# An adaLN block on one core: a new order ahead of the first exponential, and the first 512 tokens normed in two pairs

## The chip, the core and the metric

One core of a Trainium2 chip. TensorE (PE) multiplies, with its weight loads (PEld) listed apart; VectorE (DVE), ScalarE (ACT) and GpSimd (POOL) do the rest; SyncE (SP) issues the DMA transfers, one after the other in the order of the program. Each engine works through its own instructions in order. The metric is the device time of one execution in microseconds (us), compared as medians of several runs.

## What is computed

One transformer block for 2048 tokens of 512 values in float32, with 32 heads of 16 and a feed-forward width of 1792. Cut to what matters:

```python
mod = (_silu(c) @ w_mod).reshape(c.shape[0], 6, 1, -1)
sa, ca, ga, sb, cb, gb = (mod[:, 0], mod[:, 1], mod[:, 2], mod[:, 3], mod[:, 4], mod[:, 5])
h = _layernorm(x, axis=-1) * (1 + ca) + sa
x = x + ga * _A_ref(h, A_wqkv, A_wo)      # softmax attention over all tokens
h = _layernorm(x, axis=-1) * (1 + cb) + sb
x = x + gb * _B_ref(h, B_w1, B_b1, B_w2)  # dense, mish, dense
```

## The kernel before

Products in the projections are made in three parts: each float32 operand is split into a high part (rounded to the format that PE takes at full rate) and a low part (the rest), and high x high, high x low and low x high are added. `hi_copy` (L91 to L95) makes the high part on ACT, DVE or POOL; `lo_sub` (L98) subtracts to get the low part. `mm3` queues the three groups of products of one unit, `mm_go` (L129) issues one of them on PE.

*Prologue, one block of 512 tokens (tb) after the other.* x comes in as 16 tiles of 128 tokens (`xt`, L334). `stats_tb` takes mean and variance of four tiles on DVE (L371, L372) and makes the scale and shift `rs` on POOL (L373 to L376; L375 is the inverse square root as a power). `apply_tb` norms the four tiles on ACT (L382). `tr_tb` transposes them on PE, column by column of 128 values (L388: column k of all four tiles goes to one PSUM bank), applies the modulation `modc`, and writes the high part `h_h` (ACT, L391), the full value `hf` (DVE, L392) and the low part `h_l` (L98). `modc` comes from products of `w_mod` with the activated condition (L400, L404, L406) and two small DVE instructions (L410, L411). The weights stand in slices of 128 columns for queries (kind 0) and keys (kind 1) and 256 for values (kind 2); `slice_load` loads one (L231), `slice_split` splits it. `qk_unit` makes keys or queries of one slice for 512 tokens: 12 products 512 wide. Its `fin` splits the result and stores it to DRAM scratch (L269 for queries, three transfers; L273 and L274 for keys). `v_unit` does the same for values: 12 products 256 wide per 128 tokens.

*The 20 steps ahead of the first exponential (t = -20 to -1).* Softmax needs a row maximum first. In each step `max_pair` makes two pairs of score products (four times L494) that DVE reduces (L496); the rest of the step is filled with products of the queued units by `whole_units`. A step is allowed `CREDIT` products of width 512, two of width 256 counting as one, and the count starts anew in each step. When the next unit is not ready, what is left of the credit is lost. At t = -4 the maxima of the first four heads are complete: PE transposes them (L509), ACT and DVE split them (`mh` L511, `mt` L512), and one step later four small transfers (L518) put them into rows 48 and 49 of the query tiles `qa`, which the first score products (L529) read.

*The 512 steps behind.* Each makes four score products with their exponentials (L529, L532), the products of two steps earlier with the values (L547), and four maxima of the next group of four heads (L480, L482); units of the projections and of the rest of the block fill in.

What is done when is set by hand. `at(h, f)` puts f at half step h = 2t, or 2t + 1 for the second half of a step; `plan` lists the units in their order. When a unit of the plan is finished, the split of the slice two entries on is put at the next half step, the load of the slice three entries on one or two half steps later. A unit of the plan may start four half steps after the split of its slice:

```python
queue(lambda i=i, t=t0: max(2 * t, split_at.get(i, 4 * T) + 4), lambda tag, i=i, a=a: planned(i, a, tag))
```

`early_prep` loads, splits and stores six pieces of w1 in these 20 steps (L1393, L1401). `constants` stores zeros to the scratch rows 48 and 49 and loads the bias (L417 to L419), at the end of the prologue. POOL's fills of the later key tiles (L460) wait for memory that these transfers read.

## Time and profile before

| | us |
|---|---|
| median of 3 runs | 1699.01 |
| lowest and highest | 1698.46, 1699.34 |
| the profiled execution, its own time | 1697.49 |
| its span, first to last instruction | 1695.7 |
| PE busy in the span | 1672.8 (99%) |
| DVE, ACT, POOL busy | 1437.8, 1358.3, 820.1 |
| first transpose of x on PE (L388) | 15.92 |
| first L494 (maxima) | 50.59 |
| first L529 (scores) | 105.40 |

Times within the profile count from the start of the span. A row of its timeline gives start, length, engine, line and operation, output and inputs, how many instructions were merged, and in brackets the idle time of the engine before it with what ended it.

### The profile page before, as it was taken

The page shows a single profiled execution, that of the slowest core. Times are in us where ns is not written, and L with a number is a line of the kernel's source. Part 1 is how long each engine was busy: PE and PEld are TensorE (multiplying, and loading weights), DVE is VectorE, ACT ScalarE, POOL GpSimd, SP SyncE. Part 2 cuts the span into 40 slices and gives each one's busy share as a digit, 9 for nine tenths or more (in the row PEclk, how much of TensorE's full clock was granted, in tenths as well). Part 3 has the DMA queues.
Part 4 walks back from the last instruction along what each step waited for, and adds up shares of the span by engine and source line. Part 5 has one row for each costly group of instructions (what it writes and reads, how often), then busy time and mean ns, then how long its engine had stood idle before and what let it go on. Part 6 is the DMA issues. An engine that isn't in the chain of part 4 may idle for free.

```text
span 1695.7 us, 33728 instructions
## 1 busy us (share of the span) xinstructions
PE 1672.8 (99%) x12406; PEld 924.7 (55%) x12406; DVE 1437.8 (85%) x2370; ACT 1358.3 (80%) x2612; POOL 820.1 (48%) x838
## 2 busy tenths in 40 slices
PE   7999999999999999999999999999999999999999
PEld 5755665555445455555555455555555455555587
DVE  6888888888899888888889898888889988884378
ACT  6247777777778988888888998888888988888674
POOL 6456223665413464655423564555323564555442
PEclk9999999999999999999999999999999999999999
DMA  6887546777755342534355434434354433433261
GB/s 234 237 274 193 135 127 185 232 218 212 229 170 140 100 107 75 136 80 126 81 155 148 117 74 98 134 72 134 84 142 128 130 93 77 143 107 128 77 230 62
DMA packets 114029, 238.44 MB, mean 141 GB/s; under 512 B 23824, under 2 KB 49424, under 8 KB 107912
## 3 DMA queue, kind: packets, MB, share of 16 engines
q1 hardware_dynamic: 113864, 236.28, 49.3%
q8 instruction: 98, 1.61, 0.4%
q14 instruction: 67, 0.55, 0.1%
HBM read 179.95 MB, written 51.44 MB: 136 GB/s over the span
## 4 chain that ended last, share of the span: by engine, by line
PE 91%; DVE 4%; ACT 2%; DMA 2%; issue 0%; SPq 0%; POOL 0%; ACTq 0%; DVEq 0%
PE bk L547 29%; PE ring L529 23%; PE ring L480 20%; PE bk L136 9%; PE bk L129 3%; PE ring L1156 2%; DVE mx L482 2%; PE ring L129 2%; ACT pr L532 1%; DMA xt<-in_A_x 1%; PE ring L494 1%; DMA qa<-mt 1%; PE ring L859 0%; PE ring L509 0%; DVE hf L392 0%
## 5 line engine op out<-in xcount | busy, mean ns | idle before, releaser
L482 DVE TENSOR_REDUCE mx<-ring 128x1 f32<-128x512 f32 x1968 | 1223.0, 682 | 153.1 <-PE ring L480 137.4
L532 ACT ACTIVATE pr<-ring 128x512 f32<-128x512 f32 x2048 | 1078.3, 602 | 209.1 <-PE bk L136 121.1
L480 PE MATMUL ring<-ka,qa 64*128 64x512 f32 x1968 | 818.8, 430 | 1.6 <-ACT pr L532 1.1
L529 PE MATMUL ring<-qa,ka 64*128 64x512 f32 x2048 | 760.8, 403 | 5.4 <-DMA qa<-mt 2.6
L547 PE MATMUL bk<-pr,vg 128*32 128x512 f32 x4096 | 545.1, 604 | 0.0
L480 PEld LDWEIGHTS ring<-ka,qa 64*128 64x128 f32 x1968 | 351.2, 184 | 327.8 <-DVE mx L482 251.0
L529 PEld LDWEIGHTS ring<-qa,ka 64*128 64x128 f32 x2048 | 374.1, 184 | 199.0 <-DVE mx L482 114.7
L136 PE MATMUL bk<-h,w 64*128 64x512 f32 (+1 forms) x1080 | 278.9, 391 | 0.0
L136 PE MATMUL bk<-w,a_h 64*128 64x512 f32 x632 | 210.6, 413 | 0.0
L136 PEld LDWEIGHTS bk<-h,w 64*128 64x128 f32 x1080 | 178.3, 184 | 9.5 <-ACT pr L532 1.5
L547 PEld LDWEIGHTS bk<-pr,vg 128*32 128x32 f32 x4096 | 80.7, 108 | 136.2 <-issue 126.6
L136 PE MATMUL bk<-w,a_l 64*128 64x512 f32 x316 | 124.1, 393 | 0.0
L136 PEld LDWEIGHTS bk<-w,a_h 64*128 64x128 f32 x632 | 107.0, 184 | 2.2
L915 POOL TENSOR_TENSOR y<-yd,y 128x512 f32<-128x512 f32 x44 | 56.9, 1294 | 89.4 <-ACT yd L914 84.5
L749 POOL TENSOR_SCALAR qq<-ee 128x512 f32<-128x512 f32 x25 | 15.6, 624 | 169.3 <-ACT ee L743 169.3
L765 POOL TENSOR_TENSOR qq<-qq,rr 128x512 f32<-128x512 f32 x42 | 54.3, 1292 | 83.4 <-ACT rr L759 83.3
L751 POOL TENSOR_TENSOR hb<-hb,ee 128x512 f32<-128x512 f32 x42 | 54.2, 1291 | 82.3 <-DVE ee L747 80.4
L136 PE MATMUL bk<-w,o_hl 64*128 64x512 f32 x288 | 79.1, 405 | 0.0
L98 POOL TENSOR_TENSOR a_l<-hb,a_h 128x512 fp32r<-128x512 f32 x53 | 72.1, 1361 | 4.4
L136 PEld LDWEIGHTS bk<-w,a_l 64*128 64x128 f32 x316 | 58.3, 184 | 2.4
L136 PE MATMUL bk<-h_h,wl 64*128 64x512 f32 x168 | 57.7, 425 | 0.0
L95 POOL TENSOR_SCALAR qh<-qf 128x512 fp32r<-128x512 f32 x27 | 16.8, 622 | 82.8 <-ACT qf L259 56.3
(210 smaller groups left out, 1909.0 us busy)
## 6 DMA issues: line engine op xcount, KB each, us to landing
ka<-kscr SPq DMA_DIRECT2D x124, 384.0 KB
w<-w2scr SPq DMA_DIRECT2D x56, 512.0 KB
w<-w1scr SPq DMA_DIRECT2D x46, 512.0 KB
vg<-vscr SPq DMA_DIRECT2D x32, 552.0 KB
qa<-qscr SPq DMA_DIRECT2D x124, 100.0 KB
kscr<-qh SPq DMA_DIRECT2D x16, 512.0 KB
qscr<-qh SPq DMA_DIRECT2D x32, 256.0 KB
w2scr<-hl SPq DMA_DIRECT2D x14, 512.0 KB
```

Source lines behind the costliest of these rows:

```text
L98: (nc.gpsimd if eng == "p" else nc.vector).tensor_sub(lo, src, hi.bitcast(F32))
L129: nc.tensor.matmul(acc, l, r, start=start, stop=stop)
L136: i = nc.tensor.matmul(acc, l[64 * g:64 * g + 64], r[64 * g:64 * g + 64], start=start and not then, stop=bool(stop and then))
L480: nc.tensor.matmul(pm, qt[64 * s:64 * s + 64, qs * P:(qs + 1) * P], kt[64 * s:64 * s + 64, kb * TB:(kb + 1) * TB], start=True, stop=True)
L482: nc.vector.tensor_reduce(out=mxs[n][:, s, 4 * j + qs, kb:kb + 1], in_=pm, op=ALU.max, axis=AX.X)
L529: nc.tensor.matmul(p_, kt[64 * s:64 * s + 64, kc * P:(kc + 1) * P], qt[64 * s:64 * s + 64, :], start=True, stop=True)
L532: e = nc.scalar.activation(pr, p_, AF.Exp, scale=SCALE)
L547: nc.tensor.matmul(accs[n][32 * h:32 * h + 32, :], vgs[n][:, o:o + 32], pts.pop((t, h)), start=(kc == 0), stop=(kc == 15))
L751: (nc.vector if tail else nc.gpsimd).tensor_mul(hb, hb, ee)
L765: nc.gpsimd.tensor_mul(qq, qq, rr)
L915: nc.gpsimd.tensor_add(y[i], yd, y[i])
L1156: nc.tensor.matmul(po[i // 2][:, i % 2, :], l[:, s], w[:, r, :], start=(f == 0 and j == 0), stop=(f == FT - 1 and j == 2))
```

## The change

Four things move; the numbers of the computation stay the same.

1. `whole_units` carries its credit from step to step (`owed`), 7.4 a step instead of 7.5.
2. The plan takes the second slice of queries ahead of the second slice of keys; loads and splits of later slices get fixed half steps (`LATE_SPLIT`, `LATE_LOAD`), and a unit ahead of step 0 may start two half steps after its split. `constants` is called ahead of the blocks, and the early preparations start three half steps sooner.
3. `first_norm`, `first_apply` and `first_tr` replace `stats_tb(0)`, `apply_tb(0)` and the first transposes: scales for tiles 0 and 1, then for 2 and 3; tile 3 is normed on DVE instead of ACT; tiles 0 and 1 are transposed singly, then 2 and 3 together. The high part of the first key weights is made on POOL between the two pairs.
4. In the first block the products of keys and queries are issued in turn.

```diff
-    CREDIT = 7.5
+    CREDIT = 7.4
+    LATE_SPLIT = {3: -8, 4: 4}
+    LATE_LOAD = {3: -15, 4: -4, 5: 9}
...
-        slice_load(1, 1, pw)
+        slice_load(0, 1, pw)
...
+        def first_norm():
+
+            mv = lp.tile([P, 4, 2], F32, tag="ln_mv4", name="ln_mv4", bufs=2)
+            rs = lp.tile([P, 4, 4], F32, tag="ln_rs4", name="ln_rs4", bufs=3)
+            for h in range(2):
+                two = slice(2 * h, 2 * h + 2)
+                for i in range(2 * h, 2 * h + 2):
+                    st_ = lp.tile([P, 6], F32, tag="ln_st", name="ln_st", bufs=4)
+                    nc.vector.bn_stats(out=st_, in_=xts[i])
+                    nc.vector.bn_aggr(out=mv[:, i, :], in_=st_)
+                nc.gpsimd.tensor_scalar(rs[:, 0, two], mv[:, two, 1], 1.0, EPS, op0=ALU.mult, op1=ALU.add)
+                nc.gpsimd.tensor_scalar(rs[:, 3, two], mv[:, two, 0], -1.0, 0.0, op0=ALU.mult, op1=ALU.add)
+                nc.gpsimd.tensor_tensor(rs[:, 1, two], rs[:, 0, two], nhalf.to_broadcast([P, 2]), op=ALU.pow)
+                nc.gpsimd.tensor_mul(rs[:, 2, two], rs[:, 3, two], rs[:, 1, two])
+                if h == 0:
+                    hi_k = split_hi(1, 0)
+            return rs, hi_k
...
+        def first_apply(rs, i, eng):
+            xt = xts[i]
+            if eng == "a":
+                nc.scalar.activation(xt, xt, AF.Identity, scale=rs[:, 1, i:i + 1], bias=rs[:, 2, i:i + 1])
+            else:
+                nc.vector.tensor_scalar(xt, xt, rs[:, 1, i:i + 1], rs[:, 2, i:i + 1], op0=ALU.mult, op1=ALU.add)
+
+        def first_tr():
+            pts = [bank(("ring", "ms", "ring", "acc")[k]) for k in range(DK)]
+            for ii in ((0,), (1,), (2, 3)):
+                for k in range(DK):
+                    for i in ii:
+                        nc.tensor.transpose(pts[k][:, i * P:(i + 1) * P], xts[i][:, k * P:(k + 1) * P], ident)
+            return pts
...
-        slice_split(1, 0, lp)
-        slice_split(0, 0, lp)
-        apply_tb(0)
+        for i in range(2):
+            first_apply(rs, i, "a")
+        split_lo(1, 0, hi_k)
+        hi_q = split_hi(0, 0, "a")
+        split_lo(0, 0, hi_q)
+        first_apply(rs, 2, "a")
+        first_apply(rs, 3, "v")
...
+            if tb == 0:
+                (kw, qw) = early
+                early = [[m for k in range(DK) for m in (kw[k], qw[k], kw[DK + k])], qw[DK:]]
+            pe_queue.extend(m for e in early for m in e)
...
-        while credit > 0:
+        cur["owed"] = cur.get("owed", 0) + credit
+        while cur["owed"] > 0.49:
...
-    plan = [(-PRO, 2, 0, range(4, 16)), (-PRO, 1, 1, range(NB)), (-PRO, 0, 1, (0,)), (-PRO, 1, 2, range(NB)),
+    plan = [(-PRO, 2, 0, range(4, 16)), (-PRO, 0, 1, (0,)), (-PRO, 1, 1, range(NB)), (-PRO, 1, 2, range(NB)),
...
-                    at(h + d, lambda: slice_split(*plan[i + 2][1:3], hi_eng="p" if h > 0 else "a"))
-                    split_at[i + 2] = h + d
+                    split_at[i + 2] = LATE_SPLIT.get(i + 2, h + d)
+                    at(split_at[i + 2], lambda: slice_split(*plan[i + 2][1:3], hi_eng="p" if h > 0 else "a"))
...
-        at(3 * i - 34, lambda i=i: early_prep(i, 3 * i - 34))
+        at(3 * i - 37, lambda i=i: early_prep(i, 3 * i - 37))
```

How it moves instructions, in the built programs (line numbers of the change are its own; numbers at names tell buffers apart). SP before, around the four transfers of the maxima (L518, mt to qa):

```order
L310 DMA qa_109<-qscr 50x512 x2
L319 DMA ka_626<-kscr 48x2048 x2
L273 DMA kscr<-qh 128x2x512
L274 DMA kscr<-ql 128x512
L231 DMA wr<-in_A_wqkv 128x4x128
L273 DMA kscr<-qh 128x2x512
L274 DMA kscr<-ql 128x512
L518 DMA qa_106<-mt 2x4x128
L518 DMA qa_107<-mt 2x4x128
```

And in the change, where L576 is that transfer, L271 the query store, L275 and L276 the key store, L233 the weight load, L312 and L321 the loads of qa and ka:

```order
L271 DMA qscr<-qh 8x16x512 x2
L271 DMA qscr<-ql 8x16x512
L1461 DMA w1scr<-ep 128x512 x2
L275 DMA kscr<-qh 128x2x512
L276 DMA kscr<-ql 128x512
L312 DMA qa_109<-qscr 50x512 x2
L321 DMA ka_630<-kscr 48x2048 x2
L275 DMA kscr<-qh 128x2x512
L276 DMA kscr<-ql 128x512
L576 DMA qa_106<-mt 2x4x128
L576 DMA qa_107<-mt 2x4x128
L233 DMA wr<-in_A_wqkv 128x4x128
```

The weight load now stands behind the transfers of mt, one key store instead of two stands between the loads of ka and them, and a query store has come in some places ahead.

PE before, the last steps ahead of the first score product (L529; L494 are the maximum products that begin a step, L129 the units):

```order
L494 MATMUL ring<-ka_625,qa_108 128x512 x4
L129 MATMUL bk<-h_l,wh 128x512
L494 MATMUL ring<-ka_625,qa_108 128x512 x4
L129 MATMUL bk<-h_h,wh 128x512 x4
L129 MATMUL bk<-h_h,wl 128x512 x4
L494 MATMUL ring<-ka_625,qa_108 128x512 x4
L129 MATMUL bk<-h_l,wh 128x512 x4
L129 MATMUL bk<-h_h,wh 128x512 x4
L529 MATMUL ring<-qa_106,ka_104 128x512
```

And in the change the same three steps (L552 for L494, L131 for L129, L587 for L529):

```order
L552 MATMUL ring<-ka_629,qa_108 128x512 x4
L131 MATMUL bk<-h_h,wl 128x512 x2
L131 MATMUL bk<-h_l,wh 128x512 x4
L131 MATMUL bk<-h_h,wh 128x512
L552 MATMUL ring<-ka_629,qa_108 128x512 x4
L131 MATMUL bk<-h_h,wh 128x512 x3
L131 MATMUL bk<-h_h,wl 128x512 x4
L131 MATMUL bk<-h_l,wh 128x512
L552 MATMUL ring<-ka_629,qa_108 128x512 x4
L131 MATMUL bk<-h_l,wh 128x512 x3
L131 MATMUL bk<-h_h,wh 128x512 x4
L587 MATMUL ring<-qa_106,ka_104 128x512
```

One, eight and eight products beside the maxima have become seven, eight and seven. The step in front of them, with the transpose of the maxima, has eight in both programs.

DVE before, from the fourth tile's statistics (ln_mv_188 belongs to the first block, ln_mv_241 to the second) to those of the fifth:

```order
L371 BN_STATS ln_st<-xt 128x6
L372 BN_AGGR ln_mv_188<-ln_st 128x2
L410 TENSOR_SCALAR modc<-bk 128x4
L411 COPY modc<-bk 128x4
L371 BN_STATS ln_st<-xt 128x6
L372 BN_AGGR ln_mv_241<-ln_st 128x2
```

And in the change, with the second block's statistics in ln_mv_245:

```order
L394 BN_STATS ln_st<-xt 128x6
L395 BN_AGGR ln_mv_188<-ln_st 128x2
L419 TENSOR_SCALAR xt<-xt,ln_rs_189 128x512
L462 TENSOR_SCALAR modc<-bk 128x4
L463 COPY modc<-bk 128x4
L373 BN_STATS ln_st<-xt 128x6
L374 BN_AGGR ln_mv_245<-ln_st 128x2
```

The norm of tile 3 (L419) has come in ahead of modc and of the second block's statistics; it needs the scales of the second pair.

## The prediction

> **What bounds the kernel now.** I read the page's first line, then the busy time by stage, then the chain of waits from 90 to 110 us, then the timeline of the two stretches in which TensorE (PE) stands idle. By stage (columns: length, then busy time of PE, weight loads, DVE, ACT and POOL with their instructions, granted clock, DMA share, GB/s):

> ```profile
> span 1695.7 us, 33728 instructions
> ```

> ```profile
> 0.00:20.65 20.65, 11.41 (x48) 7.08 (x48) 8.57 (x25) 8.78 (x13) 13.93 (x37) 1.00 0.94 334
> 20.65:50.59 29.94, 28.22 (x158) 22.41 (x157) 25.95 (x41) 22.62 (x35) 17.50 (x19) 1.00 0.50 171
> 50.59:94.00 43.41, 43.41 (x265) 31.88 (x264) 38.57 (x36) 7.91 (x19) 24.79 (x23) 1.00 0.88 267
> 94.00:105.40 11.40, 9.21 (x40) 5.46 (x39) 9.45 (x9) 3.02 (x6) 5.92 (x6) 1.00 0.91 311
> ```

> The first score product (L529, the one the first exponential reads) starts at 105.40. In the built program of the change every PE instruction from that one on stands in the order of before, and ahead of it stand the same products. So PE loses no work, and all that can be won are its waits ahead of L529: 9.24 us idle while x is loaded and normed, 1.72 in the projections, none from 50.59 to 94.00, 2.19 from there on. The end of that stretch, first in the chain of waits (start, length, what), then in the timeline:

> ```profile
> 90.70 0.66 PE ring L494 x4
> 91.36 2.05 PE bk L129 x8
> ...
> 101.08 4.19 DMA qa<-mt
> ```

> ```profile
> 93.34 0.73 PE L494 MATMUL ring<-ka,qa 64*128 64x512 f32 x4
> ...
> 94.00 0.28 PE L509 MATMUL ring<-ident,mm 128*32 128x128 f32 x1
> ...
> 96.08 0.73 PE L494 MATMUL ring<-ka,qa 64*128 64x512 f32 x4
> 96.17 0.33 DVE L512 SCALAR_TENSOR_TENSOR mt<-mh,lows,ring 32x128 fp32r<-32x128 f32 x1
> ...
> 97.90 0.50 PE L494 MATMUL ring<-ka,qa 64*128 64x512 f32 x2 [0.22 <-DVE mx L496]
> 98.21 1.28 POOL L98 TENSOR_TENSOR wl<-wr,wh 128x512 fp32r<-128x512 f32 x1
> ...
> 99.53 0.38 SPq L231 DMA_DIRECT2D wr<-in_A_wqkv  x1
> 99.55 0.76 PEld L129 LDWEIGHTS bk<-h_h,wl 128*128 128x128 f32 x4 [0.45 <-POOL wl L98]
> ...
> 105.40 0.47 PE L529 MATMUL ring<-qa,ka 64*128 64x512 f32 x1 [1.96 <-DMA qa<-mt]
> ```

> The negated maxima mt are ready at 96.50, but their four transfers (L518) start at 101.08. They stand on SP behind a weight load (L231) that waits until POOL's subtraction (98.21 + 1.28 = 99.49) frees its buffer. They land at 105.27, and L529 waits for them. Two more waits lie ahead: the step at 96.08 had a single product beside its four maximum products, so PE ran into DVE at 97.90, and at 99.55 it waited for POOL's weights.

> How much is lost: from 93.34 to 105.40 are 12.06 us. In them PE does four quartets of L494 (0.66 each), 25 products 512 wide (2.05 / 8 = 0.256 each) and L509, for which the step from 93.34 to 96.08 is only some 0.03 longer than the 2.71 of a quartet and eight products: 2.64 + 6.40 + 0.03 = 9.07. **Lost: 2.99 us.**

> **Part 1, the stretch ahead of the first exponential.** With the credit carried over, the 20 steps get seven or eight products each, none only one. In the new order three quartets and 30 products stand between L509 and L529: 1.98 + 7.68 = 9.7 us. The other arm from L509: mt done 2.50 later (96.50 less 94.00), then 4.19 to land, 6.7 us. So L529 no longer waits for mt, by 3.0 us, if L518 can be issued when mt is ready. Ahead of it on SP there is now the store of one K unit only. That unit ends ten products and two quartets ahead of L509 (3.9 us), and needs an ACT copy and two POOL instructions after that, about 0.6 + 0.62 + 1.28 = 2.5 us (the last two by the rows below): ready 1.4 us ahead of L509, 3.9 ahead of mt. The weight split that PE waited for at 99.55 now stands ahead of L509 in the same step, and the half in question is first used one and a half steps behind. DVE has two reduces a step:

> ```profile
> 85.75 2.36 DVE L496 TENSOR_REDUCE mx<-ring 128x2 f32<-128x1024 f32 x2 [0.32 <-PE ring L494]
> ```

> Twenty steps are 47.2 us of DVE; PE's own work in them is 105.40 - 50.59 - 2.99 = 51.8, so DVE does not become the bound; a step with seven products, 0.66 + 1.79 = 2.45, still covers 2.36. I take the whole 2.99. Bounds: 0 if the queue gains nothing, 3.0 if all goes as here; there is no more to win.

> The zero constants (six transfers), the first early weight preparations and with them POOL's fills of ka move ahead. They lie in gaps of SP and POOL beside a PE that is busy 43.41 of 43.41 us; they cost nothing while that cover holds, and uncovered at most SP's own issue time. The split of the fourth slice moves behind the first eight exponentials, one ACT cast of about 0.6 us between exponentials (the one at 24.61 below, of twice the columns, takes 1.04); the slice is used some ten steps later. I take 0.

> **Part 2, the first 512 tokens.** The timeline of before:

> ```profile
> 11.07 3.57 PE L406 MATMUL bk<-sel,row 128*128 128x1 f32 x16
> ...
> 11.41 0.18 DVE L372 BATCH_NORM_AGGREGATE ln_mv<-ln_st 128x2 f32<-128x6 f32 x1
> ...
> 13.27 0.20 POOL L373 TENSOR_SCALAR ln_rs<-ln_mv 128x4 f32<-128x4 f32 x1 [4.52 <-DVE ln_mv L372]
> ...
> 13.70 1.03 POOL L375 TENSOR_TENSOR ln_rs<-ln_rs,nhalf 128x4 f32<-128x4 f32 x1
> ...
> 14.81 0.20 POOL L376 TENSOR_TENSOR ln_rs<-ln_rs 128x4 f32<-128x4 f32 x1
> 14.83 0.68 DVE L371 BATCH_NORM_STATS2 ln_st<-xt 128x6 f32<-128x512 f32 x1
> 14.96 2.50 POOL L98 TENSOR_TENSOR wl<-wr,wh 128x512 fp32r<-128x512 f32 x2
> 15.05 2.93 ACT L382 ACTIVATE xt<-xt,ln_rs 128x512 f32<-128x512 f32 x4 [1.10 <-DMA xt<-in_A_x]
> ...
> 17.93 0.18 DVE L372 BATCH_NORM_AGGREGATE ln_mv<-ln_st 128x2 f32<-128x6 f32 x1
> ...
> 18.55 0.78 ACT L391 ACTIVATE h_h<-ring,modc 128x512 fp32r<-128x512 f32 x1 [0.57 <-PE ring L388]
> ...
> 18.94 0.87 PEld L388 LDWEIGHTS ring<-ident,xt 128*128 128x128 f32 x4
> ...
> 20.25 1.28 POOL L98 TENSOR_TENSOR h_l<-hf,h_h 128x512 fp32r<-128x512 f32 x1 [0.32 <-DVE hf L392]
> ...
> 21.06 1.02 DVE L98 TENSOR_TENSOR h_l<-hf,h_h 128x512 fp32r<-128x512 f32 x1
> ...
> 21.79 2.92 ACT L382 ACTIVATE xt<-xt,ln_rs 128x512 f32<-128x512 f32 x4
> ...
> 24.61 1.04 ACT L91 CAST wh<-wr 128x1024 fp32r<-128x1024 f32 x1
> ...
> 26.08 0.78 ACT L391 ACTIVATE h_h<-ring,modc 128x512 fp32r<-128x512 f32 x1 [0.43 <-PE ring L388]
> ```

> And groups of like instructions (count, then busy time and mean ns):

> ```profile
> L107 POOL TENSOR_TENSOR ln_rs<-ln_rs,nhalf 128x1 f32<-128x1 f32 x16 | 8.9, 554 | 1.3
> L95 POOL TENSOR_SCALAR wh<-wr 128x512 fp32r<-128x512 f32 x6 | 3.7, 620 | 10.7 <-PE bk L136 10.7
> L98 DVE TENSOR_TENSOR h<-hf,h 128x512 fp32r<-128x512 f32 x4 | 2.8, 692 | 2.9 <-POOL h L95 2.9
> L93 DVE CAST a_h<-hb 128x512 fp32r<-128x512 f32 x3 | 1.3, 427 | 0.3
> ```

> *The pairs.* POOL's chain for four tiles runs from 13.27 to 15.01, 1.74 us, with a power of 1.03 on four columns. One column takes 0.554, so two take about 0.71 and a pair's chain 1.42. The first pair's statistics end at 11.59; its scales are ready at 11.68 + 1.42 = 13.10 instead of 15.01. Then POOL copies a weight half (0.62), and the second chain ends at 15.09, no earlier than before. PE is with L406 until 14.64; the eight transposes of tiles 0 and 1 at 0.87 / 4 = 0.22 each then fill it until 16.4. Tile 2 is normed by ACT from 15.13 to 15.9. The first column of tiles 2 and 3 can be transposed at 16.4, and the first h_h starts some 0.8 later, at 17.2 instead of 18.55: 1.3 earlier. The 16 products in turn of keys and queries follow h_h as it comes, and PE is through with them ahead of the next transposes.

> *What is late next.* The next transposes need tiles 4 to 7, and these become later. Their statistics stood at 14.83 on DVE, in a gap; now the norm of tile 3 stands in front of them, waiting for the second chain, with the two modc instructions behind it. If that norm ends at e, the statistics run from e + 0.25 for 3.28 us (14.83 to 18.11), POOL's chain takes 1.8, the four norms on ACT 2.95, the V weights' cast behind them 1.0: the next block's first h_h starts at e + 9.35. Before, it starts at 26.08. So **e = 16.73 is break-even** for that h_h; its transposes and the key and query ends behind it gain about 0.25 more, since before PE and not ACT was late there. Later than 16.73 costs one for one.

> *The price of that norm.* No row shows a DVE scale-and-shift from SBUF to SBUF. The nearest in size and place is the cast of the same shape, 0.43 us, with POOL elsewhere. But in this place POOL starts two subtractions of 1.25 each at the instant DVE is released. The row at 21.06 tells what such a neighbour does: alone that DVE subtraction takes 0.692, beside POOL's (20.25 to 21.53) it took 1.02 and ended 0.55 after POOL. Ends: not held, 15.13 + 0.43 = 15.6, where PE's own 1.0 caps the gain; held through both subtractions, 17.55 + 0.3 = 17.85, a loss of 0.9. I take held through the first only: 15.04 + 1.25 + 0.28 = 16.57, **a gain of 0.16 + 0.25 = 0.4 us**. From there to 50.59 the blocks follow each other as before (PE busy 28.22 of 29.94), so 0.4 arrives.

> [...]

> **Sum.** 2.99 + 0.4 = 3.4 us. The profiled execution took 1697.49 us for its span of 1695.7, so 1694.1 for the like of it; it is 1.5 below the median of the three runs, 1699.01, and against that median I forecast **1695.6 us**. The bound between faster and no change, 0.2%, about what a measurement of this kernel can tell, is 3.4 us as well: the forecast lies on it.

> **Rivals.**
> - *The norm on DVE is not held.* 2.99 + 1.0 = 4.0: 1695.0. For it: DVE may come first. Against: POOL's subtraction waits for nothing and starts at 14.96 in the row, ahead of ACT's 15.05. 0.25.
> - *Held through both.* 2.99 - 0.9 = 2.1: 1696.9. Against: two separate instructions leave DVE a place between. 0.10.
> - *Part 1 gives half.* mt or a weight half still comes late, since DMA is 0.88 to 0.91 busy. 1.5 + 0.4: 1697.1. 0.11.
> - *PE falls to half rate.* In the row at 18.94 a transpose takes 0.22 us, in the one below 0.12, after PE has been busy for some 4 us:

> ```profile
> 25.77 0.47 PEld L388 LDWEIGHTS bk<-ident,xt 128*128 128x128 f32 x4
> ```

>   In the change PE stands nearly idle from about 22.5 to 25, and 4 us at half rate behind that would cost 2: 1.4 in all, 1697.6. [...] 0.06.
> - *The pairs do nothing:* the block waits for tiles 2 and 3 anyway, whose scales come 0.08 later. 3.0: 1696.0. 0.05.
> - *Slower.* L518 stands behind a K store whose high half POOL may write only when the Q unit's stores, two units earlier and now ahead of it, have landed from the same buffer. Each us beyond the spare 3.0 holds PE at L529; past 6.4 us of delay the whole gain is gone, and 10 us give 1702.6. For it: POOL waited so in this stretch. Against: by 2.97 us at most.

> ```profile
> 102.47 0.62 POOL L95 TENSOR_SCALAR qh<-qf 128x512 fp32r<-128x512 f32 x1 [2.97 <-DMA kscr<-qh]
> ```

>   0.06.

> **Numbers.** The forecast's own case has 0.37, half on each side of the bound. Faster: 0.25 + 0.19 and 0.02 of the case in which the pairs do nothing, 0.46. Slower by 0.2%: 0.06. The rest, 0.48, within. The range leaves out the slower case, part of the half-rate one, and the best of the first: 1694.5 to 1697.9.

> **What would show it.** Right: L518 issued within 2 us of mt's end, no wait of PE for mt at L529, seven or eight products in every step, 51.8 us from the first L494 to L529, and the first L494 at about 50.2. The norm of tile 3 on DVE at over 1.2 us beside POOL, the statistics of tile 4 starting near 16.8, the first h_h near 17.2, the next block's first near 26. Wrong: a wait at L529 for the transfer of mt, a DVE norm of 0.5 us or of 2.5, half-rate products behind 25, or a first L494 later than 50.6.

## The result, and the profile after

| | before | the change |
|---|---|---|
| median of 16 runs, us | 1698.49 | 1695.11 |
| lowest and highest | 1696.86, 1699.98 | 1693.99, 1697.61 |
| profiled execution, its time and its span | 1697.49, 1695.7 | 1695.12, 1693.1 |
| first maxima product | 50.59 | 50.30 |
| first score product (L529, now L587) | 105.40 | 102.54 |
| first product with the values (L547, now L605) | 112.42 | 109.29 |

The ratio is 0.9981, 95% interval 0.9975 to 0.9988: 3.4 us faster, 2.0 to 4.2 by the interval. By stage the profile of the change shows (columns as in the prediction's first table):

```profile
20.00:50.30 30.30, 28.17 (x160) 21.99 (x158) 27.07 (x42) 23.23 (x36) 19.84 (x23) 1.00 0.62 190
50.30:102.54 52.24, 52.12 (x304) 37.24 (x303) 47.63 (x44) 9.84 (x22) 29.40 (x28) 1.00 0.87 274
102.54:109.36 6.82, 6.04 (x37) 2.98 (x40) 6.67 (x12) 6.32 (x13) 3.60 (x4) 1.00 0.99 321
```

The second row is the stretch from the first maxima product to the first score product: 52.24 us where it took 54.81, with PE busy for 52.12 of them. The rows around the maxima, from the timeline of the change (L570 makes mt, L576 sends it, L590 are the exponentials):

```profile
92.80 0.09 PEld L567 LDWEIGHTS ring<-ident,mm 128*32 128x32 f32 x1 [0.55 <-DVE mm L561]
...
94.92 0.33 DVE L570 SCALAR_TENSOR_TENSOR mt<-mh,lows,ring 32x128 fp32r<-32x128 f32 x1
95.31 2.79 SPq L576 DMA_DIRECT2D qa<-mt  x4
...
98.73 0.40 SPq L233 DMA_DIRECT2D wr<-in_A_wqkv  x1
...
103.04 0.59 ACT L261 COPY qf<-bk 128x512 f32<-128x512 f32 x1 [5.15 <-PE ring L538]
...
104.18 0.50 PE L587 MATMUL ring<-qa,ka 64*128 64x512 f32 x1 [0.67 <-ACT pr L590]
```

mt is ready at 95.25 and its transfers start at 95.31; L587 no longer waits for them. Two small waits are new: PE is now ahead of DVE at the transpose of the maxima (0.55), and the fourth score product waits for the first exponential, because a copy (L261) stands ahead of it on ACT. The first 27 us:

```profile
3.17 5.58 DVE L361 TENSOR_SCALAR sil_e<-sil_e 128x4 f32<-128x4 f32 x1 [1.51 <-ACT sil_e L360]
...
5.16 3.56 POOL L357 MEMSET ka<- 128x2048 f32 x2
...
15.09 1.47 DVE L419 TENSOR_SCALAR xt<-xt,ln_rs 128x512 f32<-128x512 f32 x1 [2.04 <-POOL ln_rs L399]
...
16.55 0.15 DVE L463 COPY modc<-bk 128x4 f32<-128x4 f32 x1
16.62 0.68 DVE L373 BATCH_NORM_STATS2 ln_st<-xt 128x6 f32<-128x512 f32 x1
...
16.85 0.45 PE L426 MATMUL bk<-ident,xt 128*128 128x128 f32 x1 [0.17 <-DVE modc L463]
...
19.04 0.78 ACT L439 ACTIVATE h_h<-ring,modc 128x512 fp32r<-128x512 f32 x1 [2.90 <-PE ring L426]
...
25.99 0.77 ACT L439 ACTIVATE h_h<-ring,modc 128x512 fp32r<-128x512 f32 x1
```

The norm of tile 3 (L419) takes 1.47 us, the first h_h comes at 19.04, half a microsecond later than before, and the next block's first at 25.99, 0.09 earlier. The first row is a surprise that has nothing to do with the change: an addition on 128x4 values took 5.58 us, up to the end of POOL's fills; before, the same instruction took 0.25.

From L605 on the two programs nearly keep their distance: 1482.0 us to the last product with the values before, 1482.6 in the change.

### The profile page after: what moved, and what is told of

Its sections match the earlier page's. It is cut to its first block, busy times and chain, and to the rows that moved or that the text cites. A ratio compares the mean times of both kernels' runs of the same rounds, so it can differ in the third digit from the quotient of the medians.

```text
span 1693.1 us, 33733 instructions
## 1 busy us (share of the span) xinstructions
PE 1670.7 (99%) x12406; PEld 922.2 (54%) x12406; DVE 1443.6 (85%) x2371; ACT 1356.1 (80%) x2610; POOL 822.3 (49%) x843
## 4 chain that ended last, share of the span: by engine, by line
PE 91%; DVE 4%; ACT 3%; DMA 1%; issue 1%; POOL 1%; SPq 0%; ACTq 0%; DVEq 0%; POOLq 0%
PE bk L605 29%; PE ring L587 22%; PE ring L538 20%; PE bk L138 10%; PE bk L131 3%; PE ring L131 2%; DVE mx L540 2%; PE ring L1214 2%; ACT pr L590 1%; PE ring L552 1%; DMA qa<-mt 0%; DMA xt<-in_A_x 0%; PE ring L917 0%; PE ring L567 0%; PE ring L138 0%
## 5 line engine op out<-in xcount | busy, mean ns | idle before, releaser
L590 ACT ACTIVATE pr<-ring 128x512 f32<-128x512 f32 x2048 | 1078.3, 603 | 207.8 <-PE bk L138 117.9
L587 PE MATMUL ring<-qa,ka 64*128 64x512 f32 x2048 | 760.1, 402 | 4.3 <-ACT pr L590 2.6
L605 PE MATMUL bk<-pr,vg 128*32 128x512 f32 x4096 | 545.0, 604 | 0.0
L587 PEld LDWEIGHTS ring<-qa,ka 64*128 64x128 f32 x2048 | 373.6, 184 | 199.2 <-DVE mx L540 115.2
L605 PEld LDWEIGHTS bk<-pr,vg 128*32 128x32 f32 x4096 | 80.7, 108 | 136.1 <-issue 126.6
L138 PEld LDWEIGHTS bk<-w,a_h 64*128 64x128 f32 x632 | 106.9, 184 | 2.7
L807 POOL TENSOR_SCALAR qq<-ee 128x512 f32<-128x512 f32 x25 | 15.6, 624 | 168.9 <-ACT ee L801 168.9
L97 POOL TENSOR_SCALAR qh<-qf 128x512 fp32r<-128x512 f32 x27 | 16.8, 623 | 88.7 <-ACT qf L261 69.7
```

The source lines that it names most:

```text
L138: i = nc.tensor.matmul(acc, l[64 * g:64 * g + 64], r[64 * g:64 * g + 64], start=start and not then, stop=bool(stop and then))
L587: nc.tensor.matmul(p_, kt[64 * s:64 * s + 64, kc * P:(kc + 1) * P], qt[64 * s:64 * s + 64, :], start=True, stop=True)
L590: e = nc.scalar.activation(pr, p_, AF.Exp, scale=SCALE)
L605: nc.tensor.matmul(accs[n][32 * h:32 * h + 32, :], vgs[n][:, o:o + 32], pts.pop((t, h)), start=(kc == 0), stop=(kc == 15))
```

## The experiments

Each run was timed against the kernel before on the same chip. The times on the right are of one profiled execution each (start of the first maxima product, the first score product, the first product with the values).

| run | ratio to before, 95% | maxima | score | values |
|---|---|---|---|---|
| before | 1 | 50.6 | 105.4 | 112.4 |
| the change | 0.9981 (0.9975 to 0.9988) | 50.3 | 102.5 | 109.3 |
| part 1 alone | 0.9988 (0.9980 to 0.9997) | 50.3 | 102.5 | 109.2 |
| part 2 alone | 0.9998 (0.9989 to 1.0007) | 50.3 | 106.9 | 114.7 |
| addition on ACT | 0.9983 (0.9975 to 0.9992) | 50.2 | 102.4 | 110.6 |
| the same, norm on ACT | 0.9975 (0.9965 to 0.9984) | 48.5 | 102.2 | 109.0 |
| the same, DVE norm alone | 0.9975 (0.9965 to 0.9985) | 49.3 | 101.5 | 108.2 |
| no carried credit | 0.9987 (0.9978 to 0.9996) | 50.3 | 103.9 | 110.4 |
| no tables | 1.0018 (1.0009 to 1.0027) | 50.2 | 109.1 | 117.6 |
| old split, tables of loads kept | 0.9993 (0.9985 to 1.0002) | 50.2 | 103.8 | 110.9 |
| constants and preparations back | 1.0002 (0.9993 to 1.0011) | 50.3 | 104.8 | 112.7 |
| weight load ahead of mt | 0.9980 (0.9971 to 0.9988) | 50.3 | 102.5 | 110.3 |
| mt behind a key store | 0.9994 (0.9985 to 1.0003) | 50.4 | 106.7 | 114.0 |
| three edits more | 0.9964 (0.9952 to 0.9977) | 47.7 | 100.2 | 107.2 |

### The two parts by themselves

Part 1 alone undoes the pairs; part 2 alone puts them into the kernel before.

```diff
-        rs, hi_k = first_norm()
+        stats_tb(0)
...
+        slice_split(1, 0, lp)
+        slice_split(0, 0, lp)
+        apply_tb(0)
...
-        tr_tb(0, pts=first_tr())
+        tr_tb(0)
...
```

> The change without the pairs and without keys and queries in turn: the first 512 tokens are normed, transposed and projected as before; the new plan, the carried credit and the moved constants stay. My theory (the two parts are separate and add up): first maxima product where before has it, 50.6 us; from there to the first score product 52.2 (as in the changed kernel, against 54.8), so that one at 102.8; time 2.6 to 3.0 us under before, 1695.5 to 1696. Rival (the blocks' pairs carry more than their 0.3 us, or the plan needs the blocks' new times): the stretch takes over 53.5 again and the gain is under 1.5 us.

> Before with the pairs, the single transposes and the products in turn alone; plan, credit and constants as before. My theory: first maxima product 0.3 us earlier, at 50.3; the stretch behind it keeps its 54.8 us, with the wait for the transfer of the maxima; first score product at 105.1, time 0.3 us under before. Rival A (the changed kernel was held up in its first 9 us by chance, so that the pairs are worth more): first maxima product at 49.5 or earlier where the condition's activation is not late. Rival B (the pairs only shift a wait): 50.6 and no gain.

Part 1 alone has the whole gain of the stretch: 52.2 us, the first score product at 102.5. It is 2.0 us faster than before (0.5 to 3.4), where 2.6 to 3.0 were expected; the intervals of this run and of the change overlap, so how much of the time the pairs add to part 1 stays open. Part 2 alone is worth 0.3 us, which can't be told from nothing; the wait for mt is there, longer than before (3.64 us at L585). That the first maxima product also comes at 50.3 without the pairs was not expected. The first block's products of keys and queries, first in the timeline of before:

```profile
20.72 2.06 PE L129 MATMUL ring<-h_h,wh 128*128 128x512 f32 x4
22.57 1.17 PE L129 MATMUL ring<-h_h,wl 128*128 128x512 f32 x4
...
25.45 0.60 PE L388 MATMUL ring<-ident,xt 128*128 128x128 f32 x4
```

And in the timeline of part 1 alone:

```profile
12.36 1.95 PE L454 MATMUL bk<-sel,row 128*128 128x1 f32 x16
...
14.49 0.68 DVE L373 BATCH_NORM_STATS2 ln_st<-xt 128x6 f32<-128x512 f32 x1
...
20.67 1.84 PE L131 MATMUL ring<-h_h,wh 128*128 128x512 f32 x4
22.35 1.08 PE L131 MATMUL ring<-h_h,wl 128*128 128x512 f32 x4
...
25.10 0.60 PE L434 MATMUL ring<-ident,xt 128*128 128x128 f32 x4
...
25.73 0.78 ACT L439 ACTIVATE h_h<-ring,modc 128x512 fp32r<-128x512 f32 x1
```

In both runs these products start at nearly the same time, and the next block's transposes follow them on PE. From the first of them to the first transpose it is 4.73 us before and 4.43 here, because PE reached its full rate earlier: by the clock records of the two traces at 22.7 us before and at 22.1 here. The 16 products with sel were faster too (1.95 us, 3.57 before), so that modc and the statistics of tile 4 came 0.34 us earlier; but this did not decide it, since the scales of tiles 4 to 7 were ready at 19.59 and ACT came to norm these tiles at 21.73. So in the old order the next block moves by 0.3 us with the moment at which PE gets its full rate. In the order with the pairs it doesn't: the first maxima product comes at 50.3 to 50.4 whether that moment was at 20.8 us (mt behind a key store) or at 22.7 (part 2 alone), since the norm of tile 3 decides there.

### The norm of tile 3, and who holds DVE

The first of three runs moves the addition that took 5.58 us to ACT; the second norms tile 3 on ACT as well; the third leaves that norm on DVE and lets POOL's first weight subtraction wait for it.

```diff
-        nc.vector.tensor_scalar_add(e, e, 1.0)
+        nc.scalar.activation(e, e, AF.Identity, scale=1.0, bias=ones)
```

```diff
-        first_apply(rs, 3, "v")
+        first_apply(rs, 3, "a")
```

```diff
-        split_lo(1, 0, hi_k)
+        normed = first_apply(rs, 3, "v")
+        sub = split_lo(1, 0, hi_k)
+        tc.add_manual_dep(sub.ins, normed.ins.name, ...)
```

> The change with one instruction moved: the 128x4 addition of 1 in the condition's activation goes from DVE to ACT. In the changed kernel's run this DVE instruction started at 3.17 and lasted 5.58 us, to the end of POOL's fills of the query and key tiles; before it took 0.25 at the same place. Theory (POOL's fills held it out, and this made the first products 2.5 us late, but tile 3's norm and not these products sets the next block): the first products start at 6.7 instead of 9.2, the transposes of the first tiles run before 16.6, the first h_h stands near 17.3 instead of 19.04, and still the next block's first h_h stays at 25.8 to 26.0, the first maxima product at 50.1 to 50.3, the time within 0.3 us of the change. Rival (the late products ate the pairs' gain): the next block's first h_h and the first maxima product come 0.8 us or more earlier, at 49.5.

> As the run before, and tile 3 is normed on ACT instead of DVE. Theory (the DVE norm, held 1.47 us beside POOL's subtraction, makes the statistics of tiles 4 to 7 late): their first one starts at 14.8 to 15.0 instead of 16.62, the next block's first h_h at 24.6 to 25.0 instead of 26.0, the first maxima product near 49.3, the time 1 us under the change, 1694.1. Rival A (behind the first blocks PE or ACT is the bound, the statistics are not): the statistics come earlier, but the first maxima product stays at 50.2. Rival B (ACT, now with one norm more, delays the first h_h by 0.75 and PE with it): 50.6 or later.

> The change with the addition of 1 on ACT (as two runs before) and POOL's first weight subtraction made to wait for the DVE norm of tile 3. Theory (POOL's subtraction held the norm): the norm takes 0.45 to 0.6 us instead of 1.47 and ends at 15.6; the statistics of tile 4 start at 15.7 instead of 16.58, the next block's first h_h at 25.0 instead of 25.93, the first maxima product at 49.3. Rival (a scale and shift of this form takes 1.47 us by itself): the norm ends at 16.5 as before, h_h at 25.9, first maxima product at 50.2. The time is told by neither alone: the run with the norm on ACT gained 1.7 us here and lost 1.5 of it to 3.4 us at half clock, 49.8 to 53.2, behind a wait of 1.06 us.

With the addition on ACT the first products start at 6.56, but the first h_h stays at 18.99: the theory's 17.3 was wrong, the rest of it right (next block's first h_h at 25.93, first maxima product at 50.2). The second transpose waits 2.01 us for modc, in that run's timeline:

```profile
16.80 0.45 PE L426 MATMUL bk<-ident,xt 128*128 128x128 f32 x1 [2.01 <-DVE modc L463]
```

The columns of x go in turn into PSUM banks, and the bank of the second column still holds the product that modc is made from; modc stands behind tile 3's norm on DVE. With that norm on ACT the first h_h starts at 17.20. The rows of the DVE norm, with POOL waiting (timeline of the third run):

```profile
15.02 0.55 DVE L420 TENSOR_SCALAR xt<-xt,ln_rs 128x512 f32<-128x512 f32 x1 [2.04 <-POOL ln_rs L399]
...
15.62 0.68 DVE L373 BATCH_NORM_STATS2 ln_st<-xt 128x6 f32<-128x512 f32 x1
...
24.99 0.77 ACT L440 ACTIVATE h_h<-ring,modc 128x512 fp32r<-128x512 f32 x1
```

0.55 us alone, 1.47 beside POOL's subtraction: the subtraction held it. From the first statistics of tile 4 to the next block's first h_h it is 9.37 us in the change, 9.37 here and 9.40 with the norm on ACT (14.74 to 24.14), so nearly each microsecond of that norm is one of the first maxima product: 50.2, 49.3, 48.5.

Of the 1.7 us that the norm on ACT won by 48.5, 1.5 were gone by the first score product. Its timeline and its stages show where:

```profile
47.56 1.05 PE L131 MATMUL ring<-h_l,wh 128*128 128x512 f32 x2 [1.06 <-POOL h_l L100]
```

```profile
48.50:50.50 2.00, 2.00 (x12) 1.60 (x12) 1.19 (x2) 1.10 (x2) 0.62 (x1) 0.79 0.98 363
50.50:55.00 4.50, 4.50 (x28) 3.70 (x26) 3.79 (x4) 0.68 (x2) 4.50 (x4) 0.71 0.42 128
```

PE waited 1.06 us for a low half, and some 2 us later the granted clock was 0.50 for 3.4 us, 49.7 to 53.1. The change has the same wait of 1.04 at 49.31 and no such fall in its profile; it comes in some executions and not in others.

### The pieces of part 1

Six runs undo one piece each, or shift the transfers of mt.

```diff
-        cur["owed"] = cur.get("owed", 0) + credit
-        while cur["owed"] > 0.49:
+        while credit > 0:
...
```

> The change with the old count of products (each step anew, 7.4): 155 products instead of 148 in the 20 steps, none left out in any step, and one K store more ahead of the transfers of the maxima. Theory (only TensorE's idle time counts; the 7 products more are taken from later steps): the first score product 7 x 0.256 = 1.8 us later, at 104.3, no wait for the maxima there, and the time as the change within 0.5 us: 1695 to 1696. Rival (the carried credit is what gains): the K store, whose half POOL may write only when older stores have landed, stands in front of the maxima's transfers, TensorE waits for them, and the time is 1 us or more above the change.

Without the carried credit the first score product comes 1.4 us later (1.8 expected), as it must with seven products more ahead of it. The theory that they would be won back fails: from L605 to the last product with the values it takes 1482.5 us, 1482.6 in the change. The span is 1.1 us longer, the time 1.0 (the intervals overlap). The rival's K store does stand in front of the maxima: their transfers start at 98.10, 1.9 us behind mt, but by the trace's semaphore events the first of them landed at 103.31, in time for L587. Why the seven products are nearly free in the later steps is not shown.

```diff
-    LATE_SPLIT = {3: -8, 4: 4}
-    LATE_LOAD = {3: -15, 4: -4, 5: 9}
+    LATE_SPLIT = {}
+    LATE_LOAD = {}
...
-                    at(LATE_LOAD.get(i + 3, h + 7), lambda: slice_load(*plan[i + 3][1:3]))
+                    at(LATE_LOAD.get(i + 3, h + (7 if h > 0 else 2)), lambda: slice_load(*plan[i + 3][1:3]))
```

> The change without its tables of half steps for splits and loads (both empty, so the old rule): the same products in the same order, but a weight load stands on SP ahead of the query stores, long before the transfers of the maxima, and waits there for POOL's subtraction. Theory (what gains is the plan's order and the credit; at the maxima 3.0 us are spare): first score product at 102.4 to 102.8, no wait for the maxima, time as the change within 0.5 us. Rival (the tables are what takes the load out of the maxima's way): query and key stores, the loads of the second query and key tiles and the maxima's transfers all start later, TensorE waits 1 us or more in the steps or at the first score product, time 1 us or more above the change.

The rival holds. From the timeline without the tables:

```profile
87.77 1.29 POOL L100 TENSOR_TENSOR wl<-wr,wh 128x512 fp32r<-128x512 f32 x1 [2.45 <-ACT wh L93]
...
89.09 0.38 SPq L233 DMA_DIRECT2D wr<-in_A_wqkv  x1
89.52 1.23 SPq L271 DMA_DIRECT2D qscr<-qh  x2
...
95.88 0.62 POOL L97 TENSOR_SCALAR qh<-qf 128x512 fp32r<-128x512 f32 x1 [4.86 <-DMA qscr<-qh]
...
99.86 0.50 PE L131 MATMUL bk<-h_h,wh 128*128 128x512 f32 x1 [2.75 <-ACT qf L261]
...
101.55 3.75 SPq L576 DMA_DIRECT2D qa<-mt  x4
...
109.12 0.47 PE L587 MATMUL ring<-qa,ka 64*128 64x512 f32 x1 [2.05 <-DMA qa<-mt]
```

Each row releases the next. The weight load waits on SP until POOL's subtraction has read the old slice (87.77 + 1.29), the query stores behind it start at 89.52 instead of 82.77, POOL waits 4.86 us for them to land before it may write the next high part, ACT's copy waits for POOL, PE for that copy, and the maxima leave 6.2 us late. PE loses 2.75 + 2.05 us in waits, half clock follows (below), and the kernel is 6.3 us slower than the change (ratio 1.0018 less 0.9981), slower than before.

```diff
-    LATE_SPLIT = {3: -8, 4: 4}
+    LATE_SPLIT = {4: 4}
```

> The change without the fixed half step for the split of the second slice of keys' successor (the third slice of keys is split by the old rule, some 6 us earlier: ACT's cast and POOL's subtraction ahead of two units' copies); the tables of the loads stay. Theory (of the tables the loads decide, since a load that waits on SP holds every store behind it): nothing changes, first score product at 102.3 to 102.7, time within 0.5 us of the change, 6 us under the run without both tables. Rival (the split in front of the units' copies is what made the query stores late there): POOL's high part of the second unit 1.3 us later or more, the maxima's transfers late, time 1.5 us or more above the change.

With the loads kept and only the split moved back there is no wait for mt (its transfers start at 96.64), so the loads, or loads and split together, are what cost most above. The median is 2.0 us above the change, and its interval just meets the change's: that the split is worth nothing is not borne out. The one profile can't say why: its stretch is 1.4 us longer than the change's, but with half clock from 51.1 to 54.5, behind the same wait for a low half; and it has a wait of 1.11 us for the exponentials.

```diff
-        constants()
         for tb in range(NB):
...
+        constants()
-        at(3 * i - 37, lambda i=i: early_prep(i, 3 * i - 37))
+        at(3 * i - 34, lambda i=i: early_prep(i, 3 * i - 34))
```

> The change with the zero constants behind the blocks again and the six early weight preparations three half steps later, as before. Theory (they lie beside a TensorE that is busy anyway, and moving them cost and won nothing): first maxima product at 50.3, first score product at 102.3 to 102.8, time within 0.5 us of the change. Rival (the last preparation's subtraction and store now fall among the query and key stores and hold the loads of the second query and key tiles): those loads 1 us or more later, a wait in the steps or for the maxima, time 1 us or more above the change.

The rival again, and the largest surprise: with these two moves undone the whole gain is gone. From the timeline (L1461 stores a weight preparation, L321 loads a key tile):

```profile
90.42 2.15 SPq L1461 DMA_DIRECT2D w1scr<-ep  x2
...
94.97 0.95 SPq L321 DMA_DIRECT2D ka<-kscr  x2
...
98.32 2.96 SPq L576 DMA_DIRECT2D qa<-mt  x4
...
104.83 0.76 PE L587 MATMUL ring<-qa,ka 64*128 64x512 f32 x1 [2.26 <-DMA qa<-mt]
```

The last preparation's store now stands among the key stores, the key tile is loaded 3.3 us later than in the change, the transfers of mt start 3.0 us later, and L587 waits 2.26 us for them. The run moves both things at once; its rows point at the preparation, and what the zero constants do by themselves was not tested.

```diff
-        at(2 * (16 * n + 16 - PRO) + 2, put)
+        at(2 * (16 * n + 16 - PRO) + (4 if n == 0 else 2), put)
```

> The change with the four transfers of the first maxima one place further back on SP: the weight load stands ahead of them, as before the change. In the change POOL's subtraction that frees the load's buffer ends at 94.64, ahead of the maxima (95.25). Theory A (not the load's place but the late subtraction behind it cost 2 us): the maxima's transfers start at 95.4 to 95.9, no wait at the first score product, which stays at 102.5, time as the change within 0.5 us. Theory B (as the prediction put it, the load ahead of the maxima costs): they start 2 us or more later, and with 3.0 us spare a wait shows only beyond that; the first score product at 102.5 to 104.5.

With 6 in place of 4 the transfers go behind a key store and the load of the values' tile too:

> The change with the four transfers of the first maxima three places further back on SP: behind the weight load, one key store and the load of the values' tile, which the change's run issued at 98.7, 99.7 to 101.3 and 101.6. Theory (3.0 us are spare, one us of delay beyond them is one us of wait): the transfers start at 101.3 to 101.9, 6.2 us later, land 4.2 to 4.5 us behind, so the first score product waits 3.2 to 3.6 us and starts at 105.6 to 106.2; behind a wait that long TensorE runs 3.4 us or more at half clock, and the time is 3 to 4.5 us above the change, 1698 to 1699.5. Rival (what follows behind the first score product is bound by DVE or by the transfers anyway): the wait is there, but the products with the values start less than 1.5 us later than in the change.

The weight load ahead of mt costs nothing: the transfers start at 95.32, and the time is that of the change. Theory A holds; what made the load expensive before was the subtraction that it waited for, not its place alone. Behind the key store, from that run's timeline:

```profile
99.67 4.33 SPq L576 DMA_DIRECT2D qa<-mt  x4
...
106.71 0.76 PE L587 MATMUL ring<-qa,ka 64*128 64x512 f32 x1 [2.53 <-DMA qa<-mt]
```

The transfers start 4.4 us later than in the change (1.6 of it because mt itself was ready only at 96.83), and PE waits 2.53 us for them. From the first issue to L587 it is 7.0 us here, 6.5 with the preparations back, 7.6 without the tables, 4.3 before. In these stretches the DMA share was 1.01 here (99.6 to 106.7) and 0.82 before (101.1 to 105.3): of these two, the one with the fuller queues took 7.0 us and the other 4.3. The median is 2.2 us above the change, less than the 3 to 4.5 expected; the profiled execution was one of the slower ones of this kernel (1699.77 against a median of 1697.73), so its own 4.7 us can't stand for it.

### A version that goes further

Beside the addition and the norm on ACT: the low half of column 1 in the fourth block on POOL, and ACT's copy behind the first four exponentials.

```diff
-    LOV = ((1,), (), (1, 3), (1, 3))
+    LOV = ((1,), (), (1, 3), (3,))
...
-                at(h + 1, lambda fin=cur["fin"]: fin(h + 1))
+                hf = 2 if h + 1 in (-1, 0) else h + 1
+                at(hf, lambda fin=cur["fin"]: fin(hf))
```

> The change with three edits that the earlier runs point to: the addition of 1 and the norm of tile 3 on ACT; in the fourth block the low half of column 1 on POOL instead of DVE (so that DVE's full values of columns 2 and 3, and with them POOL's last low half, come earlier); the copy of the key unit that stood ahead of the first exponential put behind the first four. Theory: the wait of 1.06 us for the last low half goes, the first maxima product starts at 47.4 instead of 48.5; without that wait no half clock behind it, 52.2 us to the first score product, which starts at 99.6, no wait of 0.67 us behind it; time 3 us under the change, 1692. Rival A (the clock falls all the same): 3.4 us at half rate somewhere, time 1693.5. Rival B (the transfers, busy over 0.9 from 60 to 100 us, are the next bound): waits for DMA in the steps or at the first score product, which is not under 101; time 1694 or more.

The ratio is 0.9964 (0.9952 to 0.9977): 6.1 us under before and about 2.9 under the change, though the two were not timed side by side and their intervals just touch. From its timeline:

```profile
46.73 1.05 PE L131 MATMUL ring<-h_l,wh 128*128 128x512 f32 x2 [0.32 <-POOL h_l L100]
...
92.30 0.33 DVE L570 SCALAR_TENSOR_TENSOR mt<-mh,lows,ring 32x128 fp32r<-32x128 f32 x1
...
95.85 2.78 SPq L576 DMA_DIRECT2D qa<-mt  x4
...
100.16 0.47 PE L587 MATMUL ring<-qa,ka 64*128 64x512 f32 x1 [0.20 <-DMA qa<-mt]
...
101.31 0.50 PE L587 MATMUL ring<-qa,ka 64*128 64x512 f32 x1 [0.20 <-ACT pr L590]
```

The waits of 1.06 and 0.67 us have become 0.32 and 0.20, and no half clock shows in this execution. The first maxima product is at 47.7 (47.4 expected), the first score product at 100.2 (99.6 expected): mt is ready at 92.63, but SP issues it only at 95.85, and PE waits again, 0.20 us. What holds SP, from its waits between 90 and 104 us:

```profile
SPq L576 <- DMA kscr<-qh: 2.4, 1, 2.4
```

In the traces of before and of the change the 1014 transfers on SP use eight semaphores in turn to tell of their landing, and each from the ninth on starts only after the one eight places earlier, with the same semaphore, has landed, the closest 0.015 us behind its last event. Here that is a key store issued at 86.47, whose last event the trace has at 95.77. The transfers are the next bound, as rival B had it, but the cost is smaller: it expected the first score product not under 101 and a time of 1694 or more, and the run shows 100.2 and 1693.57.

## Why the prediction was right, point by point

*The total.* 3.4 us were forecast, 3.38 measured between the medians; 1695.6 us against 1695.11. That they agree so closely is luck: the interval goes from 2.0 to 4.2, and the two profiled executions differ by 2.4 us. The sum held, its terms less well: the profile shows 2.57 us in the stretch instead of 2.99, 0.29 ahead of it instead of 0.4, and 0.27 behind the first score product, which the prediction did not count (2.86 us there, 3.13 at the first product with the values). Behind that product 0.6 us are lost again.

*"I take the whole 2.99."* The mechanism is right, the term was 0.42 too large. From the first maxima product to the transpose of the maxima the change takes 42.50 us, before 43.41. It has five products fewer there, 1.28 us, so 42.13 were due; the 0.37 more is the new wait at L567. The step ahead of the transpose has seven products instead of eight, 2.45 us by the prediction's prices, and there DVE has 2.36 us of reduces and 0.34 for mm.

*"L518 can be issued when mt is ready", with 3.0 us to spare.* It was, 0.06 us behind. But the spare was worked out from a single landing time of 4.19 us. By the trace's semaphore events the first transfer took 5.77 us to land in the change, at 101.08, so the spare ahead of L587 was 1.46 us and not 3.0. In the other runs the same transfer took from 4.17 us (the version that goes further) to 7.44 (no tables).

*The cause.* The prediction gave part 1 to the carried credit and to the weight load's place behind mt, and took the moves of the constants and of the preparations as costing nothing. Their cost was right, their worth was missed: undone, they take back 3.6 us. The place of the load is worth nothing by itself, the tables 6.3, the credit about 1.0. The pieces don't add up to the gain. A likely reason is that any of them that puts a late store or a waiting load ahead of mt spends the same spare time: the first transfer lands at 103.31 without the carried credit, at 104.70 with the preparations back and at 108.99 without the tables, against 101.08. The step that was wrong although the total came out is to cost a move by the engine that it lies beside, and not by the queue that it leaves.

*The rival on the slow side* (a store on SP that waits for older stores through POOL) is not what the change does; it is what the change without its tables does, link by link, at 6.3 us.

*The pairs.* The pair's chain takes 1.42 us and the power on two columns 0.72, as worked out. Tile 3's norm was to be held through POOL's first subtraction and end at 16.57; it ended at 16.56, and the next block's first h_h came 9.43 behind it (9.35 forecast). That POOL would hold an instruction of this form was taken over from the two-input subtraction at 21.06; the runs show it for this form, 0.55 us with POOL waiting and 1.47 beside its subtraction. "The first h_h at 17.2" was wrong by 1.8 us: the transposes of tiles 0 and 1 could not fill PE until 16.4, because the second one needs the bank that modc is read from, and modc had moved behind the norm. (In the change's own profile the late addition kept PE with the products with sel until 16.2 as well; the run with the addition on ACT shows that the bank alone is enough.) The prediction followed the tiles and the engines, and left the banks out. It cost nothing, since the next block hangs on the statistics of tiles 4 to 7.

*0.4 for part 2* was 0.29 in this profile. It is 0.3 against an execution of before in which PE reached its full rate at 22.7 us, and nothing in the profile of part 1 alone, where it did so at 22.1.

*Half rate.* The prediction put it behind 25 us, after a nearly idle stretch, with 0.06; how much idle time brings it no run shows. There it did not come. But half clock was in the profile of before all along, behind the wait for mt, and the prediction did not look for it:

```profile
107.90:108.40 0.50, 0.50 (x3) 0.41 (x2) 0.50 (x2) 0.50 (x3) 0.00 (x0) 0.64 0.71 168
108.40:111.00 2.60, 2.60 (x13) 2.14 (x13) 2.60 (x6) 1.78 (x5) 0.00 (x0) 0.50 0.76 260
111.00:111.40 0.40, 0.40 (x5) 0.40 (x4) 0.40 (x2) 0.36 (x1) 0.00 (x0) 0.50 0.87 138
```

The seventh figure, the granted clock, is 0.50 up to 111.4. DVE is busy throughout (2.60 of 2.60 us in the second row), so most of it was hidden: from the first score product to the first with the values it is 7.02 us before, 6.75 in the change. Half clock was not peculiar to this execution: of the 88 executions of before that were timed beside the experiments 3 have a mean granted clock of 1.000, of the 16 of the change 7. So less time at half clock is probably a part of the gain that the sum does not have; how large a part was not measured.

## What to carry to other kernels

On a queue that issues in order, price a move by what stands behind it: a load that waits for its buffer, or a store among stores, delays everything later on that queue, and the spare time at the end of the chain is one budget that all such moves spend. Take landing times from several stretches of the trace, the fullest among them, and not from the one row at hand: here they went from 4.2 to 7.4 us. Ahead of an instruction that is moved, look for the bank or buffer that the engine behind it needs, and look at waits of PE of about one microsecond first, since behind waits of 0.73 to 3.64 us stood 3.4 or 6.8 us at half clock (in some executions only).

## What the runs showed of the hardware

| run | wait of PE, its end | at 0.50 |
|---|---|---|
| before | 1.96, 105.40 | 108.0 to 111.4 |
| addition on ACT | 1.21, 104.59 | 106.9 to 110.3 |
| the same, norm on ACT | 1.06, 47.56 | 49.7 to 53.1 |
| weight load ahead of mt | 0.73, 104.24 | 106.7 to 110.1 |
| old split | 1.05, 49.21 | 51.1 to 54.5 |
| no tables | 2.75, 99.86 | 100.3 to 103.7 |
| no tables | 2.05, 109.12 | 110.5 to 117.3 |
| constants and preparations back | 2.26, 104.83 | 104.6 to 111.4 |
| mt behind a key store | 2.53, 106.71 | 106.1 to 112.9 |
| part 2 alone | 3.64, 106.91 | 108.0 to 114.9 |
| mt behind a key store | 1.04, 49.41 | 51.5 to 54.9 |
| weight load ahead of mt | 2.07, 386.16 | 386.6 to 390.0 |

The same wait of about 1.05 us near 49 had it behind it in three executions and not in the others, the change's among them, and one of 1.59 us at 386 (addition on ACT) had not. The waits in the table were 0.73 to 3.64 us long. What decides whether half clock follows a wait is not shown. By the clock records of before the stretch from 108.04 to 111.45 lasted 3.413 us, and the one at 1.00 ahead of it, from 22.71, lasted 85.33, 25 times as long. In the other traces too the falls and rises lie whole multiples of 3.413 us apart, as 106.69, 110.11, 386.59 and 390.00 in the run with the weight load ahead of mt: 1, 81 and 1 times.

*The clock at the start.* Five executions show 6.8 us at 0.50 between 13.6 and 22.7 us (part 1 alone: 15.3 to 22.1). In the other nine the column reads 1.00 there, but their clock records begin only at 18.9 to 22.7 us, so that figure says nothing: in before, whose record begins at 22.7, four products took 2.06 us at 20.72 and the next four 1.17.

*DVE shut out through many POOL instructions.* The 128x4 addition that starts at about 3.2 us, beside seven fills by POOL that stand back to back, took 0.25, 0.25 and 0.44 us in three executions and 5.36 to 5.58 in seven, up to the end of the last fill. In the timeline of before, with the same start as in the change:

```profile
3.17 0.25 DVE L359 TENSOR_SCALAR sil_e<-sil_e 128x4 f32<-128x4 f32 x1 [1.51 <-ACT sil_e L358]
```

In the seven it was shut out not for one instruction but until POOL's row was through: in the change it ended at 8.75, the last fill at 8.72. What decides whether it is hit is open. The prediction's argument that two separate POOL instructions leave DVE a place between is therefore not safe, though tile 3's norm did get that place: it ended at 16.56, and the two subtractions took from 15.01 to 17.69.
